# Four edits to the opening of a fused attention and feed-forward kernel: how the global index is spread, where the first scores stand, how the first feed-forward steps are cut, and where batch 1 is turned

## The chip, the core and the metric

The kernel runs on one core of a Trainium2 chip. A core has five engines that each work through their own list of instructions in order: TensorE (PE, matrix products; its weight loads are shown as PEld), VectorE (DVE), ScalarE (ACT), GpSimd (POOL) and SyncE (SP, which here only issues DMA transfers). They meet at semaphores. The metric is device time in microseconds (us); lower is better. The time before is 401.11 us, the median of four runs (398.67 to 401.29).

## What is computed

The reference is an attention with a window and a few global positions, then a gated feed-forward. Batch, heads, sequence and head size are 8, 8, 576 and 64.

```python
mask = np.abs(pos[:, None] - pos[None, :]) <= 32
is_global[global_idx] = True                        # 8 positions of 576
mask = mask | is_global[:, None] | is_global[None, :]
scores = np.where(mask, q @ k.T / sqrt(64), -1e9)
x = softmax(scores) @ v                             # as 4608 tokens x 512
g, val = x @ w_gate, x @ w_val                      # 512 -> 1536
ffn = (gelu(g) * val) @ w_out                       # 1536 -> 512
out = x + sigmoid(x @ w_res) * ffn
```

All inputs are float32 and `global_idx` is int64; the kernel multiplies in bf16 and accumulates in float32.

## The kernel before

**Tiling.** The 4608 tokens are cut into nine chunks of 512 (`NCH`), each of four token tiles of 128. A chunk is also eight windows of 64 queries, of which nine make a batch. For each chunk the feed-forward has twelve steps (`NFF`), one for each 128 columns of the hidden size: `ffn_in(c, j)` multiplies `xt` (the chunk with its features on the partitions) by a piece of `wg_t` and of `wv_t` into two PSUM banks (line 605), ACT takes the Gelu (611) and DVE multiplies and writes `ht` (612). Then `ffn_out` makes for each token tile the gate `r_ps` (623) and the product `f_ps` with `wo_t` in three thirds (648).

**Attention.** A window's scores are `kt` times `qt` (512, helper `heads`), ACT's exp writes `pt` (519, `weigh`), and `local_values` multiplies `pt` by `ve` or `vo`, the values of even and odd windows (552). `values` adds the part of the global keys, `gt` times `vgs` (564), and DVE divides into `xtok` (570 to 578). `turn_x` transposes a token tile of `xtok` on PE and copies it to `xt` (587, 588). `values` works on two banks of the pool `psm` where `split(c, t)` holds, else on the one two-bank tile of `psn`. The global rows take `kgz` and `qgz` (global keys and queries), `global_scores` (464, 469), `global_exp` (475 to 478), and `global_rows` (487 to 494), which ends in `vgs`.

**The opening.** For batches 0 and 1 keys and queries are loaded as float32, cast to `k_st` and `q_st`, and turned on PE by `turn_pair(b, p, what)` for head pairs p = 0 to 3 and for the tail of the sequence (p = -1); PE transposes (443) and DVE (k) or ACT (q) copies the result out (448, 450). For batch 0 the global columns are picked by products with one-hot tiles (`pick`, 409), and `spread_picked` (415) puts them into `kgz` and `qgz`. `first_scores(quad, pp)` adds the window mask by a product with `ident_big` (501) and then makes the scores. The index `global_idx` is loaded by ACT's queue into `gia` on all 128 partitions (line 173), copied to `gall` by DVE (312), and from there come `gpc`, `idx` (which GpSimd's gathers use, 320), `hot` and the one-hot tiles.

**Loads and casts.** The weights come as 20 pieces of 512 KB through staging slots (`load_piece`, issued by SP at 142) and are cast by GpSimd (`cast_piece`, 145). Several slots are tiles of batch 1 that are not yet in use. SP issues in this order: raw q and k of batch 0, v of batch 0 (185), ten pieces, two more, raw q and k of batch 1 (163, 167), two pieces, v of batch 1, six pieces. GpSimd casts in the same order and between the last pieces shifts v of batch 1 on chip (`shift_on_chip`, 107 and 108).

**Order.** The order of the work on each engine is written out by hand: the list from line 668 on for chunk 0, then the loop over chunks, in which `if c == 0` ... `elif j == ...` puts other work between the twelve steps. Buffers come from rotating pools: `psm` has four PSUM banks, `pss` two, `psn` one tile of two. An instruction waits where it stands, and what is behind it on its engine waits too. Before the change, the first two feed-forward steps of chunk 0 are split into two halves of 256 tokens (736 to 745); batch 1's turns stand after steps 8 to 11, two of them together after step 11 (796 to 798); `double_qk` and `turn_globals` of batch 1 stand after steps 2 and 3.

Of the kernel before, what the change touches and what calls it, by code (L numbers as in the profile page):

```python
# [8 lines left out]
F32 = mybir.dt.float32  # L9
# [14 lines left out]
def kernel(  # L24
# [129 lines left out]
    ht32 = ht.rearrange("p a b -> p (a b)").bitcast(F32)  # L154
    wo32 = wo_t.rearrange("p a b -> p (a b)").bitcast(F32)
    raw = [{"q": ht32, "k": wo32}, {"q": vraw.rearrange("p a b -> p (a b)"), "k": wo32}]
    gia = const.tile([128, 2 * NG], I32, name="gia", tag="gia")
    g32 = global_idx.bitcast(I32)

    def load_raw(b, what, p, eng):  # L160
# [9 lines left out]
    for p in (0, 1, -1, 2, 3):  # L170
        load_raw(0, "k", p, nc.sync)
        if p == 0:
            nc.scalar.dma_start(gia, bass.AP(tensor=g32.tensor, offset=g32.offset, ap=[[0, 128], [1, 2 * NG]]))
        load_raw(0, "q", p, nc.scalar if p in (0, 1) else nc.sync)

    def v_rows(c):
# [129 lines left out]


    idx = const.tile([128, B // 2], I32, name="idx", tag="idx")
    gall = const.tile([128, NG], F32, name="gall", tag="gall")
    mine8 = const.tile([128, NG], F32, name="mine8", tag="mine8")  # L310
    gpc = const.tile([128, 1], F32, name="gpc", tag="gpc")
    nc.vector.tensor_copy(gall, view(gia, 0, 128, 0, [[2, NG]]))
    nc.vector.tensor_tensor(mine8, gall, low8, ALU.mult)
    nc.vector.reduce_sum(gpc, mine8, axis=mybir.AxisListType.X)
    nc.vector.scalar_tensor_tensor(idx[:, 0:1], hrow, float(S), gpc, ALU.mult, ALU.add)
# [164 lines left out]
    def global_rows(b):  # L480

        e = b % 2
        sn = psn.tile([128, 2, 512], F32, name="sn", tag="nd")
        for c in range(-1, 5):
            for p in range(NP):
                if c < 0:
                    nc.tensor.matmul(sn[32 * p:32 * p + 32, 0, 0:2 * VG], own[e][:, 32 * p:32 * p + 32],
                                     view(vgb, 0, 128, (b // 2) * VG, [[0, 2], [1, VG]]), start=True, stop=False)
                else:
                    nc.tensor.matmul(sn[32 * p:32 * p + 16, 0, 0:2 * VG], ptg[e][:, c, 16 * p:16 * p + 16],  # L490
                                     ve[e][:, c, 2 * p:2 * p + 2, :], start=False, stop=(c == 4))
        nc.vector.tensor_tensor(view(vgs, 0, 128, e * H * VG, [[2 * VG, NP], [VG, 2], [1, VG]]),
                                view(sn, 0, 128, 0, [[0, NP], [VG, 2], [1, VG]]),
                                view(head8, 0, 128, 0, [[2, NP], [1, 2], [0, VG]]), ALU.mult)
# [40 lines left out]
        return mask  # L535

    def split(c, t):
        return c == 0 and t != 2

    def local_values(c, t):  # L540
        if split(c, t):
# [46 lines left out]
        (nc.vector.tensor_copy if c or t == 3 else nc.scalar.copy)(mine, tx)  # L588


    def ffn_in(c, j):
        steps = ffn_steps(c, j)
        for what in "gv":
            steps[what](0, 512)
        steps["end"]()

    def ffn_steps(c, j):
# [89 lines left out]
    first_scores(0, 0)  # L687
    for p in (-1, 2, 3):
        for what in "kq":
            turn_pair(0, p, what)  # L690
        for what in "kq":
            pick(p, what)
        if p < 0:
            ACT(found_end, isg[:, 0, 320:448])
    spread_picked()
    sg, ss = global_scores(0)
    row_masks()
    for c in range(2):
        cast_v(0, c, POOL)
    POOL(vo[0][64:128, 0:1, :, :], ve[0][0:64, 1:2, :, :])  # L700
    DVE(vo[0][0:64, 0:2, :, :], ve[0][64:128, 0:2, :, :])
    global_exp(0, sg, ss)
    first_scores(0, 1)
    cast_v(0, 2, POOL)
    POOL(vo[0][64:128, 1:2, :, :], ve[0][0:64, 2:3, :, :])
    for c in (3, 4):
        cast_v(0, c, POOL)
    spread_v(0, 1)
    first_scores(1, 0)
    POOL(vo[0][64:128, 2:4, :, :], ve[0][0:64, 3:5, :, :])  # L710
    first_scores(1, 1)
    begun_v = [local_values(0, t) for t in range(2)]
# [15 lines left out]
        load_piece(n)  # L728
    values(0, 0, begun_v[0])
    values(0, 1, begun_v[1])  # L730
    turn_x(0, 0)
    values(0, 2)
    turn_x(0, 1)
    values(0, 3)
    begun = [ffn_steps(0, j) for j in range(2)]
    begun[0]["g"](0, 256)
    begun[0]["v"](0, 256)
    turn_x(0, 2)
    begun[1]["g"](0, 256)
    turn_x(0, 3)  # L740
    begun[1]["v"](0, 256)
    for steps in begun:
        for what in "gv":
            steps[what](256, 512)
        steps["end"]()

    for c in range(NCH):
# [7 lines left out]
        held = None  # L755
        for j in range(NFF):
            if c or j > 1:
                ffn_in(c, j)
            if c == 0:
                if j == 0:  # L760
                    mask_rows(0, NW)
                elif j == 1:
                    mask_rows(NW, NWM)
                    zero_k(1)
                elif j == 2:
                    zero_gt(1, nc.vector)
                    zero_globals(1)
                    for n in range(1, B // 2):
                        nc.vector.tensor_single_scalar(idx[:, n:n + 1], idx[:, 0:1], float(2 * H * S * n), ALU.add)
                    double_qk(0, 1)  # L770
                elif j == 3:
                    got = turn_globals(0, 1)
                    for what in "kq":
                        DVE(compact[what][:, 0:1, :], got[what])
                elif j == 4:
                    spread_qk(1, compact, 0, {"k": DVE, "q": ACT})
                elif j == 5:
                    zero_v(1, nc.vector)
                    for p in (0, 1, 2, 3, -1):
                        for what in "kq":  # L780
                            cast_pair(1, p, what, POOL)
                    load_vraw(1)
                    for n in (14, 15):
                        load_piece(n)
                    for n in (12, 13):
                        cast_piece(n, POOL)
                    for c5 in range(5):
                        cast_v(1, c5, POOL)
                    for n in range(16, 20):
                        load_piece(n)  # L790
                    for i, n in enumerate(range(14, 20)):
                        cast_piece(n, POOL)
                        if i % 2:
                            shift_on_chip(i // 2)
                    shift_on_chip(3)
                for p in {8: (0,), 9: (1,), 10: (2,), 11: (3, -1)}.get(j, ()):
                    for what in "kq":
                        turn_pair(1, p, what)
            elif b < B:
                if c % 2 == 1:  # L800
                    n0, n1 = b // 2, b // 2 + 1
                    if j == 8:
                        double_qk(n0, n1)
                    elif j == 9:
                        got = turn_globals(n0, n1)
                        for what in "kq":
                            DVE(compact[what][:, n0:n1, :], got[what])
                        spread_v(n0, n1)
                if j == 8:
                    shift_v(b)  # L810
                    if b + 1 < B:
                        load_qk(b + 1)
                if j == 9:
                    spread_qk(b, compact, (b // 2) * 128, {"k": DVE, "q": DVE})
                if j == 11:
                    held = global_scores(b)
# [89 lines left out]
```

## Time and profile before

| | |
|---|---|
| median of four runs | 401.11 us (398.67 to 401.29) |
| the profiled execution | 398.9 us |
| its span, first to last instruction | 397.2 us |
| granted TensorE clock | 1.000 |
| DVE, ACT, POOL busy | 51%, 42%, 43% of the span |
| moved by DMA | 52.79 MB, mean 133 GB/s |
| chain that ended last | PE 80%, DMA 11%, POOL 3% |

Busy time by stretch, from the profile:

| us from the start | PE busy | DVE | ACT | POOL | DMA GB/s |
|---|---|---|---|---|---|
| 0 to 6 | 0.00 | 2.94 | 3.18 | 3.03 | 150 |
| 10 to 16.5 | 5.49 | 4.95 | 3.73 | 5.02 | 228 |
| 20 to 24 | 2.71 | 1.60 | 3.95 | 3.32 | 349 |
| 24 to 30 | 5.65 | 3.69 | 2.43 | 4.72 | 385 |
| 30 to 40 | 9.58 | 7.95 | 3.91 | 8.00 | 368 |
| 40 to 54 | 12.57 | 7.53 | 7.38 | 9.85 | 233 |
| 54 to 66 | 10.98 | 8.65 | 7.69 | 9.88 | 303 |
| 75 to 397 | 314.85 | 153.97 | 127.90 | 115.57 | 99 |

In a row of the timeline stand the start in us, the duration in us, the engine, the line of the kernel, the operation, what is written and what is read, with partitions and elements. In brackets follows for how long the engine was idle before it and what ended that. In the page's 40 slices each digit is the busy share of a slice in tenths. The chain that ended last is followed back from the last instruction; its rows have a start, a duration and a name.

### The profile page before, as it was taken

Reading aid. Unit: us, or ns where it says so; the run is one execution under the profiler, and the core shown is the slowest. Engines: PE = TensorE matmul, PEld = TensorE weight load, DVE = VectorE, ACT = ScalarE, POOL = GpSimd, SP = SyncE. Lnnn points to the kernel's source line nnn. Section 1 sums busy time; section 2 is a strip of 40 time slices with the busy share of each in tenths; the row PEclk is TensorE's granted clock in tenths of the full one; section 3 lists DMA queues with packets and bytes.
Section 4 is the critical chain, followed back from the end, with each engine's and each line's share of the span. In section 5 each row is a group of like instructions: output and inputs, shape, how many; then the busy total and the mean of one; then the engine's idle time right before and its main releaser. Section 6 shows DMA issues by size and latency. Waiting matters only on the chain.

```text
span 397.2 us, 8378 instructions
## 1 busy us (share of the span) xinstructions
PE 376.6 (95%) x3275; PEld 196.5 (49%) x3326; DVE 202.7 (51%) x444; ACT 168.6 (42%) x279; POOL 171.6 (43%) x207
## 2 busy tenths in 40 slices
PE   2889989999999999999999999999999999999995
PEld 1664545444544455445544554455445544554443
DVE  6857558435734464356444553665445534553322
ACT  5663484236433542345334623372337333633320
POOL 6777679768147613561297126712501210121011
PEclk9999999999999999999999999999999999999999
DMA  7999999999939982999399929993990310031002
GB/s 202 230 370 368 250 306 227 182 149 167 89 102 124 199 87 80 142 171 109 81 134 181 116 79 118 190 99 84 111 148 21 88 53 2 2 92 55 0 29 79
DMA packets 153144, 52.79 MB, mean 133 GB/s; under 512 B 136528, under 2 KB 143568, under 8 KB 153104
## 3 DMA queue, kind: packets, MB, share of 16 engines
q1 hardware_dynamic: 77024, 41.88, 46.5%
q0 software_dynamic: 75392, 9.84, 41.3%
q8 instruction: 26, 0.43, 0.5%
q10 hardware_dynamic: 688, 0.53, 0.5%
q14 instruction: 14, 0.11, 0.1%
HBM read 39.20 MB, written 9.44 MB: 122 GB/s over the span
## 4 chain that ended last, share of the span: by engine, by line
PE 80%; DMA 11%; POOL 3%; SPq 2%; issue 2%; ACT 1%; DVE 0%; DVEq 0%; POOLq 0%
PE v_ps L605 21%; PE f_ps L648 21%; PE g_ps L605 20%; PE r_ps L623 6%; PE nd L552 4%; DMA extra<-in_moe_w_val_dram 3%; DMA xtok<-in_moe_w_val_dram 2%; DMA vraw<-in_moe_w_out_dram 2%; PE sc L512 2%; DMA extra<-in_moe_w_res_dram 2%; PE nd L564 2%; SPq L185 2%; DMA wo_t<-in_k_dram 2%; PE ss L469 1%; POOL wo_t L145 1%
## 5 line engine op out<-in xcount | busy, mean ns | idle before, releaser
L612 DVE SCALAR_TENSOR_TENSOR ht<-gsb,v_ps 128x512 bf16<-128x512 bf16 x108 | 74.3, 688 | 99.5 <-PE v_ps L605 91.4
L611 ACT ACTIVATE gsb<-g_ps 128x512 bf16<-128x512 f32 x108 | 64.5, 597 | 127.3 <-PE g_ps L605 115.7
L654 POOL TENSOR_TENSOR ob<-prb,xtok 128x512 f32<-128x512 f32 x35 | 40.3, 1152 | 175.4 <-DVE prb L652 173.2
L605 PE MATMUL v_ps<-xt,wv_t 128*128 128x512 bf16 (+1 forms) x440 | 111.2, 375 | 0.5
L605 PE MATMUL g_ps<-xt,wg_t 128*128 128x512 bf16 (+1 forms) x422 | 108.8, 375 | 0.6
L648 PE MATMUL f_ps<-wo_t,ht 128*128 128x512 bf16 x395 | 98.1, 379 | 1.8 <-issue 0.8
L605 PEld LDWEIGHTS <-wv_t 128*128 128x128 bf16 x440 | 43.0, 98 | 50.2
L605 PEld LDWEIGHTS <-wg_t 128*128 128x128 bf16 x440 | 42.6, 98 | 48.8 <-DVE xt L588 0.4
L648 PEld LDWEIGHTS <-ht 128*128 128x128 bf16 x420 | 38.8, 98 | 38.6
L626 ACT ACTIVATE rsb<-r_ps 128x512 bf16<-128x512 f32 x36 | 21.7, 607 | 71.0 <-PE r_ps L623 69.9
L519 ACT ACTIVATE pt<-sc 128x512 bf16<-128x512 f32 x72 | 37.4, 624 | 4.4 <-PE sc L512 4.4
L652 DVE SCALAR_TENSOR_TENSOR prb<-rsb,f_ps 128x512 f32<-128x512 bf16 x35 | 24.0, 686 | 28.0 <-PE f_ps L648 25.6
L623 PE MATMUL r_ps<-wr_t,xt 128*128 128x512 bf16 x136 | 36.2, 379 | 0.5
L534 DVE TENSOR_TENSOR pt<-pt,maskw 128x512 bf16<-128x512 bf16 x64 | 29.0, 468 | 8.3 <-ACT pt L519 6.3
L91 POOL DMA_DIRECT2D q_st<-in_q_dram x25 | 21.4, 862 | 19.5 <-DMA qt<-q_st 19.4
L552 PEld LDWEIGHTS <-pt 128*128 128x128 bf16 x576 | 22.1, 97 | 9.3 <-issue 0.9
L99 POOL DMA_DIRECT2D ve<-in_v_dram x30 | 25.4, 864 | 0.0
L577 DVE TENSOR_TENSOR xtok<-nd,rden 128x512 bf16<-128x512 f32 x33 | 22.8, 691 | 1.3
L91 POOL DMA_DIRECT2D k_st<-in_k_dram x25 | 21.1, 856 | 5.4 <-DMA kt<-k_st 4.7
L552 PE MATMUL nd<-ve,pt 128*128 128x65 bf16 x320 | 22.7, 193 | 0.1
L576 DVE RECIPROCAL rden<-nd 128x8 f32<-128x8 f32 x33 | 6.8, 207 | 28.1 <-PE nd L564 27.9
L623 PEld LDWEIGHTS <-xt 128*128 128x128 bf16 x144 | 13.4, 97 | 15.1
(162 smaller groups left out, 299.4 us busy)
## 6 DMA issues: line engine op xcount, KB each, us to landing
out_dram<-ob SPq DMA_DIRECT2D x35, 256.0 KB
vo<-ve SPq DMA_DIRECT2D x12, 260.0 KB
q_st<-in_q_dram POOLq DMA_DIRECT2D x20, 128.0 KB, 5.3
k_st<-in_k_dram POOLq DMA_DIRECT2D x20, 128.0 KB, 6.5
ve<-in_v_dram POOLq DMA_DIRECT2D x18, 128.0 KB, 7.6
wo_t<-in_k_dram SPq DMA_DIRECT2D x8, 256.0 KB
vraw<-in_q_dram SPq DMA_DIRECT2D x8, 256.0 KB
extra<-in_moe_w_out_dram SPq DMA_DIRECT2D x4, 512.0 KB
```

Source lines behind the costliest of these rows:

```text
L91: nc.gpsimd.dma_start(dst[0:n, r, :].rearrange("p (h d) -> p h d", d=D), src[b].rearrange("h s d -> s h d")[128 * r:128 * r + n])
L99: nc.gpsimd.dma_start(t[p0:p1, c, :, 0:D], v[b].rearrange("h s d -> s h d")[s0 + p0:s0 + p1])
L519: nc.scalar.activation(mine, sc, ACTF.Exp, bias=0.0, scale=SCALE)
L534: nc.vector.tensor_tensor(m, m, view(maskw, 0, 128, 64 * i0, [[0, 2], [64, 4], [1, 64]]), ALU.mult)
L552: nc.tensor.matmul(nds[h // 4][:, VG * (h % 4):VG * (h % 4) + VG], view(pt, 0, 128, c0, [[1, 128]]), vw, start=(h % 4 == 0 and e == 0), st ...
L605: nc.tensor.matmul(held[what][:, c0:c1], w[:, kk, 128 * j:128 * j + 128], x[:, kk, c0:c1], start=(kk == 0), stop=(kk == NKT - 1))
L611: nc.scalar.activation(gsb, held["g"], ACTF.Gelu, bias=0.0, scale=1.0)
L612: nc.vector.scalar_tensor_tensor(ht[:, j, :], gsb, 0.5, held["v"], ALU.mult, ALU.mult)
L623: nc.tensor.matmul(r_ps, xt[c % 2][:, kk, 128 * t:128 * t + 128], wr_t[:, kk, :], start=(kk == 0), stop=(kk == NKT - 1))
L648: nc.tensor.matmul(held["f"], ht[:, j, 128 * t:128 * t + 128], wo_t[:, j, :], start=(j == 0), stop=(j == NFF - 1))
L652: nc.vector.scalar_tensor_tensor(prb, held["r"], 1.0, held["f"], ALU.add, ALU.mult)
L654: nc.gpsimd.tensor_tensor(ob, prb, xtok[c % 2][:, t, :], ALU.add)
```

## The change

It has four parts. The index is loaded as one row of 64 bytes; two masks split each value into its low three bits and the rest, DVE casts both to bf16 (each is exact there), and two products with the first row of `sel`, which is all ones, add them up on all 128 partitions. `first_scores(1, 0)` moves up, behind the turn of the tail; for pair 3 the picks and `spread_picked` stand before the turn; the row masks and the copy of the global values change places; `global_rows(0)` takes its bank from `pss`, and tiles 1 and 3 of chunk 0 use the tile of `psn`. Steps 0 and 1 of chunk 0 are made a token tile at a time: all four products of tile t follow directly on `turn_x(0, t)`. In the loop of chunk 0 the turns of batch 1 stand one after each of steps 7 to 10 and the last between the two products of step 11; the casts of the global keys and queries stand after step 4 and their transposes after step 6, and `zero_v` after step 3.

```diff
--- before.py
+++ after.py
@@ -154,7 +154,7 @@
     ht32 = ht.rearrange("p a b -> p (a b)").bitcast(F32)
     wo32 = wo_t.rearrange("p a b -> p (a b)").bitcast(F32)
     raw = [{"q": ht32, "k": wo32}, {"q": vraw.rearrange("p a b -> p (a b)"), "k": wo32}]
-    gia = const.tile([128, 2 * NG], I32, name="gia", tag="gia")
+    gia = const.tile([1, 2 * NG], I32, name="gia", tag="gia")
     g32 = global_idx.bitcast(I32)
 
     def load_raw(b, what, p, eng):
@@ -170,7 +170,7 @@
     for p in (0, 1, -1, 2, 3):
         load_raw(0, "k", p, nc.sync)
         if p == 0:
-            nc.scalar.dma_start(gia, bass.AP(tensor=g32.tensor, offset=g32.offset, ap=[[0, 128], [1, 2 * NG]]))
+            nc.scalar.dma_start(gia, bass.AP(tensor=g32.tensor, offset=g32.offset, ap=[[2 * NG, 1], [1, 2 * NG]]))
         load_raw(0, "q", p, nc.scalar if p in (0, 1) else nc.sync)
 
     def v_rows(c):
@@ -306,10 +306,18 @@
 
 
     idx = const.tile([128, B // 2], I32, name="idx", tag="idx")
+    gs = const.tile([1, 2, NG], I32, name="gs", tag="gs")
+    g2 = const.tile([1, 2, NG], BF16, name="g2", tag="g2")
     gall = const.tile([128, NG], F32, name="gall", tag="gall")
     mine8 = const.tile([128, NG], F32, name="mine8", tag="mine8")
     gpc = const.tile([128, 1], F32, name="gpc", tag="gpc")
-    nc.vector.tensor_copy(gall, view(gia, 0, 128, 0, [[2, NG]]))
+    for n, keep in enumerate((7, 1023 - 7)):
+        nc.vector.tensor_single_scalar(gs[:, n, :], view(gia, 0, 1, 0, [[2, NG]]), keep, ALU.bitwise_and)
+    nc.vector.tensor_copy(g2, gs)
+    gp = psm.tile([128, NG], F32, name="gp", tag="mm")
+    for n in range(2):
+        nc.tensor.matmul(gp, sel[0:1, :], g2[:, n, :], start=(n == 0), stop=(n == 1))
+    nc.vector.tensor_copy(gall, gp)
     nc.vector.tensor_tensor(mine8, gall, low8, ALU.mult)
     nc.vector.reduce_sum(gpc, mine8, axis=mybir.AxisListType.X)
     nc.vector.scalar_tensor_tensor(idx[:, 0:1], hrow, float(S), gpc, ALU.mult, ALU.add)
@@ -480,14 +488,17 @@
     def global_rows(b):
 
         e = b % 2
-        sn = psn.tile([128, 2, 512], F32, name="sn", tag="nd")
+        if b:
+            sn = psn.tile([128, 2, 512], F32, name="sn", tag="nd")[:, 0, 0:2 * VG]
+        else:
+            sn = pss.tile([128, 2 * VG], F32, name="sn", tag="sc")
         for c in range(-1, 5):
             for p in range(NP):
                 if c < 0:
-                    nc.tensor.matmul(sn[32 * p:32 * p + 32, 0, 0:2 * VG], own[e][:, 32 * p:32 * p + 32],
+                    nc.tensor.matmul(sn[32 * p:32 * p + 32, :], own[e][:, 32 * p:32 * p + 32],
                                      view(vgb, 0, 128, (b // 2) * VG, [[0, 2], [1, VG]]), start=True, stop=False)
                 else:
-                    nc.tensor.matmul(sn[32 * p:32 * p + 16, 0, 0:2 * VG], ptg[e][:, c, 16 * p:16 * p + 16],
+                    nc.tensor.matmul(sn[32 * p:32 * p + 16, :], ptg[e][:, c, 16 * p:16 * p + 16],
                                      ve[e][:, c, 2 * p:2 * p + 2, :], start=False, stop=(c == 4))
         nc.vector.tensor_tensor(view(vgs, 0, 128, e * H * VG, [[2 * VG, NP], [VG, 2], [1, VG]]),
                                 view(sn, 0, 128, 0, [[0, NP], [VG, 2], [1, VG]]),
@@ -535,7 +546,7 @@
         return mask
 
     def split(c, t):
-        return c == 0 and t != 2
+        return c == 0 and t % 2 == 0
 
     def local_values(c, t):
         if split(c, t):
@@ -588,10 +599,12 @@
         (nc.vector.tensor_copy if c or t == 3 else nc.scalar.copy)(mine, tx)
 
 
-    def ffn_in(c, j):
+    def ffn_in(c, j, between=None):
         steps = ffn_steps(c, j)
         for what in "gv":
             steps[what](0, 512)
+            if what == "g" and between:
+                between()
         steps["end"]()
 
     def ffn_steps(c, j):
@@ -687,26 +700,33 @@
     first_scores(0, 0)
     for p in (-1, 2, 3):
         for what in "kq":
-            turn_pair(0, p, what)
+            if p == 3:
+                pick(p, what)
+            else:
+                turn_pair(0, p, what)
+        if p == 3:
+            spread_picked()
         for what in "kq":
-            pick(p, what)
+            if p == 3:
+                turn_pair(0, p, what)
+            else:
+                pick(p, what)
         if p < 0:
             ACT(found_end, isg[:, 0, 320:448])
-    spread_picked()
+            first_scores(1, 0)
     sg, ss = global_scores(0)
-    row_masks()
     for c in range(2):
         cast_v(0, c, POOL)
     POOL(vo[0][64:128, 0:1, :, :], ve[0][0:64, 1:2, :, :])
     DVE(vo[0][0:64, 0:2, :, :], ve[0][64:128, 0:2, :, :])
+    spread_v(0, 1)
+    row_masks()
     global_exp(0, sg, ss)
     first_scores(0, 1)
     cast_v(0, 2, POOL)
     POOL(vo[0][64:128, 1:2, :, :], ve[0][0:64, 2:3, :, :])
     for c in (3, 4):
         cast_v(0, c, POOL)
-    spread_v(0, 1)
-    first_scores(1, 0)
     POOL(vo[0][64:128, 2:4, :, :], ve[0][0:64, 3:5, :, :])
     first_scores(1, 1)
     begun_v = [local_values(0, t) for t in range(2)]
@@ -728,20 +748,21 @@
         load_piece(n)
     values(0, 0, begun_v[0])
     values(0, 1, begun_v[1])
+    begun = [ffn_steps(0, j) for j in range(2)]
+
+    def begin(t):
+        for steps in begun:
+            for what in "gv":
+                steps[what](128 * t, 128 * t + 128)
+
+    values(0, 2)
     turn_x(0, 0)
-    values(0, 2)
-    turn_x(0, 1)
     values(0, 3)
-    begun = [ffn_steps(0, j) for j in range(2)]
-    begun[0]["g"](0, 256)
-    begun[0]["v"](0, 256)
-    turn_x(0, 2)
-    begun[1]["g"](0, 256)
-    turn_x(0, 3)
-    begun[1]["v"](0, 256)
+    begin(0)
+    for t in range(1, 4):
+        turn_x(0, t)
+        begin(t)
     for steps in begun:
-        for what in "gv":
-            steps[what](256, 512)
         steps["end"]()
 
     for c in range(NCH):
@@ -755,7 +776,7 @@
         held = None
         for j in range(NFF):
             if c or j > 1:
-                ffn_in(c, j)
+                ffn_in(c, j, (lambda: [turn_pair(1, -1, what) for what in "kq"]) if c == 0 and j == 11 else None)
             if c == 0:
                 if j == 0:
                     mask_rows(0, NW)
@@ -767,15 +788,16 @@
                     zero_globals(1)
                     for n in range(1, B // 2):
                         nc.vector.tensor_single_scalar(idx[:, n:n + 1], idx[:, 0:1], float(2 * H * S * n), ALU.add)
+                elif j == 3:
+                    zero_v(1, nc.vector)
+                elif j == 4:
                     double_qk(0, 1)
-                elif j == 3:
+                elif j == 6:
                     got = turn_globals(0, 1)
                     for what in "kq":
                         DVE(compact[what][:, 0:1, :], got[what])
-                elif j == 4:
                     spread_qk(1, compact, 0, {"k": DVE, "q": ACT})
                 elif j == 5:
-                    zero_v(1, nc.vector)
                     for p in (0, 1, 2, 3, -1):
                         for what in "kq":
                             cast_pair(1, p, what, POOL)
@@ -793,9 +815,9 @@
                         if i % 2:
                             shift_on_chip(i // 2)
                     shift_on_chip(3)
-                for p in {8: (0,), 9: (1,), 10: (2,), 11: (3, -1)}.get(j, ()):
+                if 7 <= j < 11:
                     for what in "kq":
-                        turn_pair(1, p, what)
+                        turn_pair(1, j - 7, what)
             elif b < B:
                 if c % 2 == 1:
                     n0, n1 = b // 2, b // 2 + 1
```

In the listing of each engine's instructions SP and POOL keep their order. PE has 68 more instructions: the two products of the index and 32 more of the first two steps, each with its weight load. DVE has two more rows and ACT the same work in another order.

## The prediction

> **What bounds the kernel now.** I read the page first (engine shares, 40 slices, the chain that ended last), then the chain in order of time up to 76 us, then the timeline to 75 us.
>
> ```profile
> span 397.2 us, 8378 instructions
> PE 376.6 (95%) x3275; PEld 196.5 (49%) x3326; DVE 202.7 (51%) x444; ACT 168.6 (42%) x279; POOL 171.6 (43%) x207
> PE   2889989999999999999999999999999999999995
> DMA  7999999999939982999399929993990310031002
> ```
>
> After 75 us the kernel is matrix work back to back (PE busy 314.85 of 322.00 us there) and the change touches none of it, so all that can move is the moment at which PE gets there. Before 75 us the 16 DMA engines are full too. The chain in order of time says which of the two ends last:
>
> ```profile
> 17.08 9.05 DMA xtok<-in_moe_w_val_dram
> 26.19 11.18 DMA extra<-in_moe_w_val_dram
> 39.88 7.38 DMA extra<-in_moe_w_res_dram
> 52.13 8.59 DMA vraw<-in_moe_w_out_dram
> 60.77 1.05 POOL wo_t L145
> 66.39 0.63 POOL vo L108
> 67.02 0.59 PE f_ps L648 x2
> ```
>
> The loads set the pace to 60.7 us, GpSimd's casts and shifts from there to 67.0, and only then PE. PE itself is close behind that: it starts the last values tile of chunk 1 (which reads what L108 shifted) at 67.69, 0.67 us after POOL was done at 67.02. That gap is how much PE can gain if loads and POOL stay put. Other edges are looser: the last `wo_t` cast ends at 65.60, its product starts at 66.57 (0.97 to spare).
>
> The places that the change touches, from the timeline:
>
> ```profile
> 4.75 0.17 DVE L312 CAST gall<-gia 128x8 f32<-128x8 int32 x1 [1.69 <-DMA gia<-in_global_idx_dram]
> 10.57 1.01 PE L501 MATMUL sc<-xt,ident_big 128*128 128x512 bf16 x2
> 17.40 0.59 PE L501 MATMUL sc<-xt,ident_big 128*128 128x512 bf16 x2
> 20.41 0.61 POOL L190 CAST ve<-vraw 96x512 bf16<-96x512 f32 x1 [1.14 <-DMA vraw<-in_v_dram]
> 21.97 0.70 DVE L492 TENSOR_TENSOR vgs<-sn,head 128x520 bf16<-128x520 f32 x1 [2.28 <-PE sn L490]
> 22.73 0.61 PE L564 MATMUL nd<-vgs,gt 128*128 128x260 bf16 x4 [0.81 <-DVE vgs L492]
> 25.70 0.58 ACT L588 COPY xt<-tx 128x512 bf16<-128x512 bf16 x1 [0.51 <-PE tx L587]
> 28.77 0.33 PEld L605 LDWEIGHTS <-wg_t 128*128 128x128 bf16 x4 [0.36 <-DVE xt L588]
> 34.51 0.10 PEld L399 LDWEIGHTS <-kgd 128*128 128x128 bf16 x1 [0.86 <-DVE kgd L389]
> 51.15 0.38 PE L443 MATMUL tk<-ident,k_st 128*128 128x128 bf16 x4 [0.67 <-ACT qt L450]
> 52.70 0.31 PE L464 MATMUL sg<-qt,kgz 128*32 128x288 bf16 x4 [0.60 <-ACT qt L448]
> ```
>
> In brackets stands the idle time before an instruction and what ended it. DVE waits for the index; PE waits for the global rows (0.81), for a turned tile (0.36), for a cast on DVE, and twice for ACT when batch 1 is turned.
>
> **Index row.** Removed: 127 of 128 rows of 64 bytes. Added: two masks of 1x8 and one cast on DVE, two 8-column products on PE, and the copy now reads PSUM. The landing of one row isn't in the trace. Upper bound: as now, 4.75. Lower: the last output piece takes 1.71 us from issue to landing, and the index is issued by 1.23, so 2.94. The Trainium skill (DMA: Bandwidth & Descriptors, Anatomy of one DMA) puts a fixed 2.0 us on a transfer, an estimate of 3.23 here. DVE is free at 3.06, so row or rule differ by 0.17 us at most; I take 3.06. The small steps of this chain follow each other at 0.20 (4.75, 4.95, 5.15), a second mask adds 0.08: cast at 3.34, PE at 3.55, product about 0.2, copy at 3.8 instead of 4.75. So 0.95 us sooner; if the row lands as late as now, 0.75 later. Behind that wait on DVE stand all masks and the first k cast (7.21), on POOL the gathers. What follows: q's last pair is cast at 12.93 as its load lands, and v's last piece at 20.41, also a load. So the 0.95 is mostly swallowed. The index rows also trickle through the ramp of the loads (31, 138, 269 GB/s in the three 0.75 us slices from 2.25 us, against 381 after): without them the whole stream of loads may be 0 to 0.7 us ahead; I take 0.3.
>
> **First scores reordered.** Eight exps, the same products, other places. Scores of quad 1, half 0, move from 18.3 us to about 12.5. Here the trace and a rule speak against it: the two 512-column products take 1.01 us at 10.57 and 0.59 at 17.40. TensorE: Matmul & The Clock Gate (Part 1) says that the array runs at half rate until about 3.4 us of sustained activity. Issue to issue the moved block costs 0.95 + 0.54 us early and 0.87 late (18.27 to 19.14), so 0.6 more than it saves, unless PE would wait there anyway. Late, 0.87 goes from the path: `nd` could start at 19.15 instead of 20.02; but it needs the two exps behind the global exps, which end at 19.5 now. I take 19.5, 0.5 sooner. `sn` moves to another bank and ends 0.4 to 0.6 sooner; it can't end before v's last cast (21.02 now, 20.7 with the stream 0.3 ahead) plus 0.25. So the global products, 22.73 now (call that G), come 0.6 to 1.0 sooner: 0.7. On DVE the row masks (0.76 + 0.74) now stand behind the v copies; the masked `gt` is needed only at G.
>
> **A token tile at a time.** This is the cost. PE is in order, and each turn now stands directly before the steps that read it. Turn to first product takes 1.07 us by ACT (four transposes 0.39, hand-over 0.04, copy 0.58, 0.06) and 0.91 by DVE (27.86 to 28.77). 32 products of 256 columns become 64 of 128. The four transposes at 69.42 take 0.22, so 55 ns each with their weight load; the skill's page on TensorE (Back-to-back issue gap) gives about 81 ns for such pairs at 128 columns. By the row the four tiles are 4 x 0.87 = 3.5 us, as now; by the rule 5.2, 1.7 us more. I take the row. From G: global products and tile 2 to +1.2; tile 3 needs the bank that tile 1 holds until DVE is done (0.30 + 1.11 + 0.94 = +2.35), then 0.75, so tile 0's steps run +3.1 to +4.0. Then 1.07 + 0.87, 1.07 + 0.87, 0.91 + 0.87 = 5.66: step 2 starts at G + 9.65. Now it is 30.53 - 22.73 = G + 7.80. So **1.85 us lost** on PE, at G 0.7 gained: step 2 starts 1.15 later than now. Weights don't stop it: the last of the first four pieces is cast at 27.22.
>
> **Globals of batch 1 two steps later.** PE's hole is from 33.98 (step 3 done) to 34.72: 0.74, of which the two transposes are 0.11 to 0.2. The DVE casts (0.99 + 0.21) now have two steps of time. **0.55 gained.** The ones and zeros of v (0.09 + 0.28 + 0.28) only trade places on DVE; four banks cover that, and the cast that frees the buffer ends at 33.04.
>
> **Turns of batch 1.** Now: step 10 ends at 47.70, r_ps starts at 53.45, 5.75 us. After: turn 0.44, g 0.86, last turn 0.44 (+0.1 for its bank), v 0.86, ACT's tail copies 0.74 mostly under v, then 0.62 + 0.5 for the global scores: 3.75. One turn more lies before step 10: 0.44. **1.55 gained.** The casts are ready: pair 0 at 39.62, its turn not before 41.4. But ACT now does the last Gelu (0.60) behind those copies and before the table load and the exps; relative to r_ps it falls behind by 0.9 - 0.5 = 0.4, and PE already waits for ACT's exps at 57.44 (0.17). **0.4 given back**; bounds 0 and 0.6.
>
> No DMA or POOL instruction changes its place on SP or POOL.
>
> **Sum.** -0.7 + 1.85 - 0.55 - 1.55 + 0.4 = -0.55 at PE, about -0.85 if the earlier stream passes through at G in full. The lid at 67 us is 0.67 + 0.3 = 1.0. I take -0.7: the profiled execution of 398.9 (its span 397.2 and 1.7 around it) would be 398.2. The runs shown have a median of 401.11 and spread from 398.67 to 401.29, more than this whole effect, so on the median: **400.4 us**.
>
> **Rivals.** (1) The turned tiles decide (slower). If ACT's exps hold PE at 57 us whatever the turns save, the 1.55 is gone: -0.7 + 1.85 - 0.55 + 0.4 = +1.0, so 402.1. For it: three exposed copies in strict order; against: the two holes of 0.67 and 0.60 stand in the trace and have named causes. It decides once less than 0.55 of the 1.55 arrives; at 81 ns per product it would be worse, +2.7. (2) The loads move more: without index rows the stream is 0.7 ahead, POOL is done at 66.3, G comes 1.4 sooner, ACT keeps up. PE's sum is -1.4 + 1.85 - 0.55 - 1.55 = -1.65, the lid 0.67 + 0.7: -1.4, so 399.7; with the array warm one window sooner and a median near the lowest runs, 398.5. (3) It does nothing at the end: loads and casts hold PE at 67.6 as now, 401.1, within 0.3; the holes only move. Against: POOL ends 0.67 before PE.
>
> **Chances.** Small gain 0.50 (399.8 to 400.9), turned tiles 0.18, earlier stream 0.20, nothing 0.12. The range of 398.3 to 402.3 covers them but for the ends of rivals 1 and 2 and takes in the spread of the runs. Half a per cent, 2.0 us, is about what a measurement of this kernel can tell from no change. Faster by more needs rival 2 and a low median: 0.22. Slower by more needs rival 1 with dear products: 0.10. Within: 0.68.
>
> **What would show it.** `gall` at about 3.8; G near 22.0; three waits of PE of 0.7 to 0.85 us on turned tiles, with step 2 at about 31.7; no wait at the globals' transposes; r_ps near 52.3; then PE at the last values tile at 66.7 to 67.1 with POOL just done. It is wrong if the 128-column products exceed 55 ns, if ACT holds the scores of chunk 1, or if the casts land much sooner.

## The result and the profile after

| | before | after |
|---|---|---|
| median | 400.01 us (63 runs, 398.65 to 401.78) | 398.73 us (42 runs, 397.23 to 400.23) |
| ratio | | 0.9968 [0.9959, 0.9978] |
| the profiled execution | 398.9 us | 399.54 us |
| its span | 397.2 us | 397.8 us |

The change saves 1.28 us, 0.32% of the time (0.22 to 0.41%): real, and below the half per cent that the prediction called measurable. The two profiled executions point the other way by 0.64 us. Before's lies near the lower end of its runs and after's 0.8 us above its median, so spans must not be subtracted here; stages can be compared one by one. The runs of before gather near 399 and near 401 us, and the profiled one is of the first kind: of the 71 runs of before beside the experiments below, the 22 with a granted clock of 1.000 average 398.98 us and the other 49 average 400.75, while for after 12 and 32 such runs average 398.79 and 398.80, so most of the 1.28 us is gained over runs of which there is no profile.

The page of after, its first lines:

```profile
span 397.8 us, 8446 instructions
PE 377.4 (95%) x3309; PEld 197.2 (50%) x3360; DVE 202.2 (51%) x445; ACT 168.6 (42%) x279; POOL 172.1 (43%) x207
PE   3979998999999999999999999999999999999995
DMA  8999999899739972999299929993990310041002
```

The first slice (10 us) has PE at 3 and DMA at 8 tenths, where it was 2 and 7: the opening begins sooner. From 75 us on the slices look alike, but not all is equal there: chunk 1 takes 41.15 us (40.59 in before) and chunk 4 takes 41.04 (40.69), which is where nearly all of the 0.64 us the other way comes from. The account of the prediction comes back to chunk 4.

The timeline of after at the places shown of before (start, duration, engine, line; in brackets the idle time before and what ended it):

```profile
3.71 0.17 DVE L320 COPY gall<-gp 128x8 f32<-128x8 f32 x1 [0.28 <-PE gp L319]
12.29 1.04 PE L512 MATMUL sc<-xt,ident_big 128*128 128x512 bf16 x2
18.49 0.87 POOL L190 CAST ve<-vraw 96x512 bf16<-96x512 f32 x1 [0.81 <-DMA vraw<-in_v_dram]
21.66 0.61 PE L575 MATMUL nd<-vgs,gt 128*128 128x260 bf16 x4 [0.80 <-DVE vgs L503]
24.06 0.20 PE L563 MATMUL nd<-ve,pt 128*128 128x65 bf16 x1 [0.56 <-DVE xtok L588]
26.73 0.38 PE L618 MATMUL g_ps<-xt,wg_t 128*128 128x128 bf16 x4 [0.67 <-ACT xt L599]
28.68 0.38 PE L618 MATMUL g_ps<-xt,wg_t 128*128 128x128 bf16 x4 [0.67 <-ACT xt L599]
30.47 0.38 PE L618 MATMUL g_ps<-xt,wg_t 128*128 128x128 bf16 x4 [0.52 <-DVE xt L599]
39.95 0.10 PEld L407 LDWEIGHTS <-kgd 128*128 128x128 bf16 x1
51.32 0.43 PE L472 MATMUL sg<-qt,kgz 128*32 128x288 bf16 x8
53.73 0.62 PE L523 MATMUL sc<-qt,kt 64*128 64x64 bf16 x31 [0.38 <-ACT ptg L483]
```

The index is there at 3.71 instead of 4.75, v's last cast starts at 18.49 instead of 20.41 and the global products (G) at 21.66 instead of 22.73. At 24.06 PE waits 0.56 us for the bank that tile 1 of chunk 0 holds; then three turned tiles each hold PE for 0.52 to 0.67 us where before had one wait of 0.36. PE's waits for the globals' transposes and for ACT in batch 1's turns are gone; behind `r_ps` there is a new one of 0.38 for ACT's exps. Stage by stage, with the shift against before in each profiled execution:

| moment, us | before | after | shift | change within the stage |
|---|---|---|---|---|
| `gall` | 4.75 | 3.71 | -1.04 | |
| G | 22.73 | 21.66 | -1.07 | -0.03 |
| step 2 | 30.53 | 31.54 | +1.01 | +2.08 |
| `r_ps` of chunk 0 | 53.45 | 52.19 | -1.26 | -2.27 |
| first `f_ps` | 59.34 | 58.62 | -0.72 | +0.54 |
| third values tile of chunk 1, second half | 65.93 | 65.79 | -0.14 | +0.58 |
| feed-forward of chunk 1 | 74.88 | 74.74 | -0.14 | 0.00 |

Of the 1.26 us that PE is ahead at `r_ps`, 1.12 are gone fourteen microseconds later. The chain that ended last, in order of time, names the place. In after it runs through DVE's masks (`pt` times `maskw`, line 545), no longer through the loads and GpSimd:

```profile
26.09 0.59 ACT xt L599
63.47 2.28 DVE pt L545 x2
65.79 0.36 PE nd L563 x6
```

### The profile page after: what moved, and what is told of

It is laid out like the page before. It is cut to its first block, busy times and chain, and to the rows that moved or that the text cites. A ratio compares the mean times of both kernels' runs of the same rounds, so it can differ in the third digit from the quotient of the medians.

```text
span 397.8 us, 8446 instructions
## 1 busy us (share of the span) xinstructions
PE 377.4 (95%) x3309; PEld 197.2 (50%) x3360; DVE 202.2 (51%) x445; ACT 168.6 (42%) x279; POOL 172.1 (43%) x207
## 4 chain that ended last, share of the span: by engine, by line
PE 76%; DMA 7%; issue 5%; DVE 4%; POOL 4%; ACT 2%; DVEq 0%; POOLq 0%
PE v_ps L618 19%; PE g_ps L618 18%; PE f_ps L661 18%; PE r_ps L636 6%; PE nd L563 4%; DMA kgf<-in_k_dram,idx 2%; PE sc L523 2%; POOL ve L99 2%; PE nd L575 2%; DMA kt<-k_st 2%; DMA out_dram<-ob 1%; POOL ob L667 1%; DMA vgf<-in_v_dram,idx 1%; PE ss L477 1%; ACT pt L530 1%
## 5 line engine op out<-in xcount | busy, mean ns | idle before, releaser
L618 PEld LDWEIGHTS <-wg_t 128*128 128x128 bf16 x456 | 43.4, 98 | 50.3 <-issue 2.4
L563 PE MATMUL nd<-vo,pt 128*128 128x65 bf16 x256 | 20.1, 193 | 1.4 <-DVE pt L545 0.9
```

The costliest lines, as they stand in the source:

```text
L563: nc.tensor.matmul(nds[h // 4][:, VG * (h % 4):VG * (h % 4) + VG], view(pt, 0, 128, c0, [[1, 128]]), vw, start=(h % 4 == 0 and e == 0), st ...
L618: nc.tensor.matmul(held[what][:, c0:c1], w[:, kk, 128 * j:128 * j + 128], x[:, kk, c0:c1], start=(kk == 0), stop=(kk == NKT - 1))
```

## The experiments

Each kernel is after with one thing undone or added, or before with one part alone. Medians are from 6 or 12 runs (seven for the first kernel with casts on ACT); us in brackets are what the ratio differs from 1, times 400.0. The kernels ran in three groups, each with its own runs of before (medians 400.54, 399.44 and 400.60), so ratios are compared and not medians. The medians of before move more from group to group than its averages (400.26, 400.02 and 400.57), so between kernels of different groups some tenths of a microsecond can come from before itself.

**The index alone** (before with that part):

```diff
-    gia = const.tile([128, 2 * NG], I32, name="gia", tag="gia")
+    gia = const.tile([1, 2 * NG], I32, name="gia", tag="gia")
...
-    nc.vector.tensor_copy(gall, view(gia, 0, 128, 0, [[2, NG]]))
+        nc.tensor.matmul(gp, sel[0:1, :], g2[:, n, :], start=(n == 0), stop=(n == 1))
+    nc.vector.tensor_copy(gall, gp)
```

> The kernel before with the index row alone. The changed kernel measures 1.28 us less than before. If the loads set the time (its load stream stood 1.1 to 1.4 us ahead), this edit alone gives most of that: about -1.0 us, ratio 0.9975, with GpSimd's casts of the first weights 1.4 us sooner. If PE's own sum decides, as in the prediction, the index gives only what reaches the global products: -0.3 to -0.7 us, and the turns must give the rest.

398.45 us, ratio 0.995 [0.9933, 0.9967] (-2.0). At best estimate one small part alone gains more than the whole change; the intervals overlap a little.

**All but the index** (after, the same lines reversed):

> The changed kernel with the index loaded on 128 partitions as before. Loads decide: the gain is nearly gone, 0 to -0.3 us against before. PE's sum decides: turns and globals still pay for the token tiles, about -0.6 us against before.

399.93 us, ratio 0.999 [0.9972, 1.0008]. The other three parts together are worth nothing that can be told from zero. In the trace `gall` is at 4.98, G at 22.66.

How an index of 64 bytes does this stands in the DMA view from 1.5 to 5 us (40 slices of 0.0875 us: busy share of the DMA engines in tenths, then GB/s). Before, and then after:

```profile
DMA  0000000000009601242224566466689989999999
GB/s 0 0 0 1 7 2 1 2 4 3 4 15 51 38 25 51 72 85 76 73 64 144 189 202 190 165 191 202 226 294 309 342 306 363 363 375 386 375 363 375
```

```profile
DMA  0000977966338999978898899998988899989799
GB/s 0 0 1 0 47 47 117 187 187 117 117 129 293 339 374 363 328 246 281 304 328 293 304 351 398 328 363 316 328 316 304 304 351 340 304 281 293 269 316 316
```

With 128 rows of 64 bytes the keys and queries issued at the same time hardly move until 2.5 us, and 300 GB/s are passed at 4.1. With one row that is at 2.6. Half a megabyte has landed at 4.81 before and 3.68 after, 8 MB at 29.74 and 28.30, 16 MB at 56.55 and 55.16: the whole stream is 1.1 to 1.4 us ahead and stays so. Without the index part 8 MB is at 29.72, and in the profiles of all twelve kernels with the one row it is 0.9 to 2.6 us sooner than in before, so that part is the cause of the earlier stream. In addition SP's wait of 0.8 us for `gia`, which held a load of q until 4.74, is gone. Why the first packets of k come 0.6 us later beside the rows, no view shows. The same edit also brings `gall` a microsecond sooner, and no run parts the two; that the stream is what pays is argued from the chain of before, which runs through the loads.

**All but the token tiles** (after, the first two steps as before, and tile 1 and 3 in their old banks):

```diff
-        return c == 0 and t % 2 == 0
+        return c == 0 and t != 2
...
-    begin(0)
-    for t in range(1, 4):
-        turn_x(0, t)
-        begin(t)
+    begun[0]["g"](0, 256)
+    begun[0]["v"](0, 256)
+    turn_x(0, 2)
+    begun[1]["g"](0, 256)
+    turn_x(0, 3)
+    begun[1]["v"](0, 256)
```

> The changed kernel with the first two feed-forward steps in halves of 256 tokens and tiles 1 and 3 of chunk 0 on the banks of before. The prediction prices the token tiles at 1.85 us of PE. If PE ends last, this is 1.85 us faster than the changed kernel (-3.1 us against before, ratio 0.992). If GpSimd's casts and shifts and the DVE masks at 63 to 67 us are a lid, at most 0.3 us faster than the changed kernel, because that kernel already waits there.

396.26 us, ratio 0.9889 [0.9866, 0.9913] (-4.4): the fastest of all. From G to step 2 it takes 7.80 us, exactly as before and as with the index alone; after takes 9.88.

**All but the turns and globals of batch 1** (after, batch 1 as before):

```diff
-                if 7 <= j < 11:
+                for p in {8: (0,), 9: (1,), 10: (2,), 11: (3, -1)}.get(j, ()):
                     for what in "kq":
-                        turn_pair(1, j - 7, what)
+                        turn_pair(1, p, what)
```

> The changed kernel with batch 1's turns after steps 8 to 11 and its global casts and transposes after steps 2 and 3, as before. The prediction prices these two at 0.55 + 1.55 - 0.4 = 1.7 us. If PE ends last, 1.7 us slower than the changed kernel (+0.4 us against before). If the lid holds, PE has 0.6 us in hand there, so 1.1 us slower than the changed kernel (-0.2 us against before).

400.15 us, ratio 0.9997 [0.9978, 1.0016]: this part is worth 1.2 us within the change (0.3 to 2.0). `r_ps` comes at 53.80, 1.6 later than in after.

**Token tiles turned one ahead** (after):

```diff
+    turn_x(0, 1)
     begin(0)
-    for t in range(1, 4):
-        turn_x(0, t)
-        begin(t)
+    turn_x(0, 2)
+    begin(1)
+    turn_x(0, 3)
+    begin(2)
+    begin(3)
```

> The changed kernel with each turn one tile ahead: the turn of tile t + 1 stands before the products of tile t, so PE no longer waits for the copy. If the token tiles cost what they do through the three exposed copies (0.67 + 0.67 + 0.52 us of idle PE), this gives about 1.9 us against the changed kernel, ratio to before 0.992, step 2 at about 29.6 us. If it is the 128-column products themselves, or the banks of tiles 1 and 3, it gives under 0.5 us.

397.21 us, ratio 0.9943 [0.9922, 0.9965] (-2.3). The timeline of PE in this kernel, a turn and the products after it:

```profile
25.88 0.39 PE L598 MATMUL tx<-ident,xtok 128*128 128x128 bf16 x4
26.10 0.39 PE L618 MATMUL g_ps<-xt,wg_t 128*128 128x128 bf16 x4
```

Four transposes take 0.22 us and no bracket follows: all three waits are gone, and G to step 2 is 7.54 us. The products of 128 columns are not dear, 0.22 for four; it was the exposed copies. The wait of 0.56 for the bank stays. In time the gain over after is 1.0 us, with intervals that overlap a little (the medians lie 1.5 apart).

**All but the first scores** (after, the list up to the last first score as before):

```diff
         if p < 0:
             ACT(found_end, isg[:, 0, 320:448])
-            first_scores(1, 0)
...
+    spread_v(0, 1)
+    first_scores(1, 0)
```

> The changed kernel with the scores of quad 1, the picks of pair 3, the row masks and the value copy in the order of before. From the sum of the parts measured so far (index, turns, token tiles) this part is worth about nothing: within 0.5 us of the changed kernel. If the early block costs what the slow array makes of it, this is 0.6 us faster; if taking 0.87 us from in front of the values is on the path, 0.5 us slower.

400.48 us, ratio 1.0005 [0.9984, 1.0026]. By that the part is worth 1.5 us (0.6 to 2.4), but the traces do not show it: chunk 1 starts at 74.67 here and at 74.74 in after. The profiled run of this kernel, 399.27 us, is the second quickest of its twelve.

**Index and turns alone** (the two edits last named, both taken back):

> Only the index row and the turns of batch 1, with the first scores and the first steps as before. Index and turns by their own runs: -2.0 and -0.9 to -1.4 us, so about -3 us, ratio 0.9925. If the first scores are worth the 1.5 us that no_first showed, this is 1.5 us slower than the kernel without the tiles (0.9889), which also gives 0.9925; if it is 0.989 here, the first scores are worth nothing and index and turns add up to more than each alone.

396.95 us, ratio 0.9908 [0.9888, 0.9929] (-3.7). Against all but the tiles (-4.4) the first scores are worth 0.8, with an interval from -0.5 to +2.0.

These kernels make a ladder:

| parts in the kernel | us against before | the step |
|---|---|---|
| index | -2.0 | -2.0 (± 0.7) |
| index, turns and globals | -3.7 | -1.7 (± 1.1) |
| index, turns and globals, first scores | -4.4 | -0.8 (± 1.3) |
| all four | -1.3 | +3.2 (± 1.0) |

The last step compares two groups. Straight from the medians, 396.26 and 398.73, it is 2.5 us.

**Two casts of `w_out` on ACT.** What takes PE's lead back between 58 and 66 us? These runs take work from GpSimd, where the prediction had put the lid.

```diff
-                        cast_piece(n, POOL)
+                        if n < 18:
+                            cast_piece(n, POOL)
...
+            for n in (18, 19):
+                cast_piece(n, ACT)
             cast_second("k", 0, NQT, ACT)
```

> The changed kernel with the last two pieces of w_out cast by ACT, which is idle at 60 to 63 us, and not by GpSimd. In the changed kernel the masks at 63.47 take 2.27 us for two while GpSimd casts, and 0.82 for two while it is idle. If GpSimd beside DVE is what gives PE's lead back between 62 and 66 us, these masks take about 1.0 us and chunk 1's feed-forward starts about 0.6 us sooner: ratio to before 0.995. If the lead is lost elsewhere, no change against the changed kernel; ACT's later casts of k may then cost up to 0.5 us.

402.62 us, ratio 1.0073 [1.0044, 1.0102]: slower than before by 2.9. In this kernel and the next the casts stand behind the loads of batch 2, so 64 rows of one piece of `w_out` are taken from the keys of batch 2. That order is also what they cost; ACT in the timeline, and DVE's masks at the same time:

```profile
66.63 1.99 ACT L145 CAST wo_t<-extra 128x1024 bf16<-128x1024 f32 x2 [6.54 <-DMA extra<-in_k_dram]
```

```profile
64.10 0.75 DVE L545 TENSOR_TENSOR pt<-pt,maskw 128x512 bf16<-128x512 bf16 x2
```

ACT idles 6.54 us for a load, and the products wait 2.3 us for its casts. But the two masks now take 0.75 us, with GpSimd idle.

**The same without token tiles:**

> The changed kernel without the token tiles and with the last two casts on ACT. Without the tiles alone it measured 396.26 us, 0.9889 of before. In that one PE goes from the second pair of values at 59.85 to the third at 64.42, 4.57 us where the kernel before needs 3.21. If GpSimd beside DVE does that, another 0.8 to 1.2 us go: ratio 0.986. If not, 0.989.

402.44 us, ratio 1.005 [1.003, 1.0071]. The same delay; chunk 1 starts at 79.11.

**The casts on ACT ahead of those loads** (after):

```diff
+            for n in (18, 19):
+                cast_piece(n, ACT)
             for what in "kq":
                 load_second(what)
-            for n in (18, 19):
-                cast_piece(n, ACT)
             cast_second("k", 0, NQT, ACT)
```

> The changed kernel with the last two pieces of w_out cast by ACT, now ahead of the loads of batch 2 on SP. In act_casts and no_tiles_act those loads stood ahead: ACT's casts waited for them until 66.63, and 64 rows of one piece were taken from k of batch 2. If GpSimd beside DVE gives back PE's lead between 62 and 66 us, the masks at 63.5 take about 1.0 instead of 2.27 us for two and chunk 1's feed-forward starts 0.6 to 1.2 us sooner: ratio 0.994. If not, 0.9968 as the changed kernel; slower than that if ACT is late again.

398.33 us, ratio 0.995 [0.9931, 0.9968] (-2.0). Against after it is 0.7 us faster at best estimate, with intervals that overlap. What happens to the masks: before, then after, then this kernel (timelines of GpSimd, DVE and PE; line 534 of before is 545 of after):

```profile
63.31 2.29 POOL L145 CAST wo_t<-extra 128x1024 bf16<-128x1024 f32 x2
64.28 1.59 DVE L534 TENSOR_TENSOR pt<-pt,maskw 128x512 bf16<-128x512 bf16 x2
65.93 0.20 PE L552 MATMUL nd<-vo,pt 128*128 128x65 bf16 x1 [0.38 <-DVE pt L534]
```

```profile
63.25 2.22 POOL L145 CAST wo_t<-extra 128x1024 bf16<-128x1024 f32 x2
63.47 2.27 DVE L545 TENSOR_TENSOR pt<-pt,maskw 128x512 bf16<-128x512 bf16 x2
65.79 0.20 PE L563 MATMUL nd<-vo,pt 128*128 128x65 bf16 x1 [0.94 <-DVE pt L545]
```

```profile
61.95 0.61 POOL L107 COPY vo<-ve 64x520 bf16<-64x520 bf16 x1
62.61 0.71 POOL L108 COPY vo<-ve 64x520 bf16<-64x520 bf16 x1
62.19 1.42 DVE L545 TENSOR_TENSOR pt<-pt,maskw 128x512 bf16<-128x512 bf16 x2
```

DVE begins 0.81 us sooner in after than in before and is done 0.13 sooner: it ends 0.27 us after GpSimd's pair of casts in both. All the lead becomes wait at the masks. Beside two of GpSimd's copies of 0.61 and 0.71 (the last kernel) two masks take 1.42, beside two casts 2.27, beside nothing 0.75.

**The same on the two faster kernels** (without tiles, and turned one ahead):

> The same edit on the changed kernel without token tiles (0.9889 of before without it, with 1.5 us of PE waiting for masked scores at 56 to 75 us and 0.3 for a cast on GpSimd). If those waits come from GpSimd's casts, 0.8 to 1.5 us less: ratio 0.986. If not, 0.989 or more.

396.95 us, ratio 0.9907 [0.9889, 0.9926]; without ACT's casts 0.9889 [0.9866, 0.9913]: no gain. PE's longest wait from 55 us on in this kernel, next to the wait for the masks that all but the tiles has up to 75 us (what waited, for what; us in all, times, longest):

```profile
PE f_ps L661 <- POOL wo_t L145: 1.5, 1, 1.5
```

```profile
PE nd L563 <- DVE pt L545: 1.5, 2, 0.9
```

An earlier cast, still GpSimd's, takes the place of the masks as the longest wait.

> The same edit on the changed kernel with each turn one tile ahead (0.9943 of before, interval 0.9922 to 0.9965, its profiled run 394.8 us of span against 397.8). If the masks hold its lead back, 0.8 to 1.5 us less: ratio 0.991. If not, 0.994.

396.61 us, ratio 0.9909 [0.9887, 0.9931]; without ACT's casts 0.9943 [0.9922, 0.9965]. Chunk 1 starts at 71.67, the soonest of all, against 72.22. So in none of the three kernels is the gain in time from taking the two casts off GpSimd clear of the noise; what the runs show is how long the masks take.

## Why the prediction was right, and where it was not

The change of time was put at -0.7 us and is -1.28 (0.9968 [0.9959, 0.9978]), within half a per cent. The 400.4 us was reckoned from a median of four runs, 401.11; with 63 runs before is 400.01, so as a time the forecast is 1.7 us off and 398.73 lies below the likeliest case (399.8 to 400.9), while as a difference it is just inside it. Most of the signs came as listed: `gall` at 3.71 (3.8), step 2 at 31.54 (31.7), `r_ps` at 52.19 (52.3), three waits on turned tiles, none at the globals' transposes. PE's sum held too: -0.55 forecast, -0.72 at the first `f_ps`.

The match is in part luck. Two terms, one of each sign, were too small in the times, and their errors partly cancel. In the profiled pair only 0.14 us of PE's lead reaches chunk 1, because the lid was misread; where the rest of the 1.28 of the medians arises, no profile shows.

**Index: failed in size.** The path to `gall` held to the tenth: DVE's first step on the index starts at 2.99, the copy at 3.71 where 3.8 was said. The 3.23 that the fixed 2.0 us gave was too late: the row was in use at 2.99, 1.64 us after the end of its issue and 2.17 after the beginning. (The section behind the 2.0 us describes transfers that GpSimd issues; this one is ACT's.) The step that failed is "the whole stream of loads may be 0 to 0.7 us ahead; I take 0.3". It measured 1.1 to 1.4, and the index alone gives 2.0 us. The row-by-row rates of before (31, 138, 269 GB/s) had been read as a slow ramp and charged to the index only in small part; the run without the index part has the slow ramp again (`gall` at 4.98, 8 MB at 29.72). The 0.7 for G, with the first scores in it, stands against 2.8 for these two steps of the ladder. Inside the full change less of it arrives: all but the index is only 0.9 us slower than after (± 0.8).

**First scores: open.** The masks' two products at 12.29 take 1.04 us, as the row of 10.57 had said, so moving them costs PE what was charged. Their worth in time is 1.5 by one pair of kernels and 0.8 by the other, the second not distinct from zero.

**Token tiles: mechanism right, too small.** Three exposed copies at 0.67, 0.67 and 0.52, tile 3 at G + 2.40 where + 2.35 was forecast for the bank, and 2.08 us at step 2 where 1.85 was. Row against rule came out for the row: 0.22 for four products, not the 0.32 of the 81 ns in the Trainium skill (TensorE: Matmul & The Clock Gate, Back-to-back issue gap). The ladder says 3.2 (± 1.0), the medians 2.5. Of what goes beyond 2.08, part lies behind 75 us (below).

**Turns and globals: right.** -0.55 - 1.55 + 0.4 = -1.7; the ladder has -1.7, and the run without this part 1.2. In the trace step 10's end to `r_ps` takes 3.66 us (3.75 forecast, 5.75 before), and 0.54 is given back before `f_ps` (0.4 forecast), 0.38 of it in the new wait for ACT's exps.

**The lid: right place, wrong reading.** "That gap is how much PE can gain if loads and POOL stay put", 0.67, is wrong. PE does not end at GpSimd's shifts but at DVE's masks, which share the time with GpSimd's casts; it already waited 0.38 for them in before, a bracket that the prediction did not read. With casts at the same moment (63.25 and 63.31) PE gained 0.14 of the 1.26 it was ahead, the same 0.13 by which the masks were done sooner. The Trainium skill has a rule for it (SBUF — State Buffer, Who interferes with whom): a DVE instruction with two inputs in SBUF waits out a GpSimd instruction that reads SBUF. The rows agree: two masks take as long as the two casts or copies beside them (2.27 and 2.22; 1.42 and 0.61 + 0.71), and 0.75 when GpSimd is idle. That the shared port is the reason is the page's account; the rows show the durations only. How much this costs in an execution hangs on when the loads bring the last casts. In the profile of after this pair starts at 63.25, for the second piece of `w_out` came late:

```profile
57.02 1.04 POOL L145 CAST wo_t<-extra 128x1024 bf16<-128x1024 f32 x1 [1.41 <-DMA extra<-in_moe_w_out_dram]
```

In all but the turns that cast stands at 53.73. With the index alone the pair starts at 60.42: it falls beside the masks of the tile before (1.99 us for two), and PE's waits for masks come to 0.68, against 0.94 in after and 0.38 in before. So this one execution shows little of the gain that the runs measure; how the others lie cannot be seen.

**Behind 75 us: a term put at nothing.** The prediction said that the change touches nothing after 75 us, "so all that can move is the moment at which PE gets there". That does not hold. In the profiles of all eight kernels with token tiles PE stands still in chunk 4, always before the same product, the last of the global scores, which reads keys that a DMA has turned. The hole is 0.2 to 1.2 us long. In the six kernels without token tiles, before among them, there is none. Chunk 4 takes 40.86 to 41.86 us in the eight and 40.69 or 40.70 in the six. From after, the product, then two lines of the DMA view from 210 to 214 us (slices of 0.1 us):

```profile
219.10 0.26 PE L477 MATMUL ss<-qgz,kt 128*128 128x16 bf16 x4 [0.20 <-DMA kt<-k_st]
GB/s 95 184 269 416 170 179 20 10 8 23 3 79 287 292 156 360 151 148 145 150 154 143 148 151 195 205 229 246 219 119 9 10 9 8 10 9 10 128 151 145
q8 instruction: 1, 0.02, 1.7%
```

The last line is one load of 16 KB of instructions. It starts at 211.56, takes 1.08 us, and soon after it the DMA engines move next to nothing for 0.7 us (8 to 10 GB/s from 213.0), while the keys are being turned. (The pause before it, at 210.6, follows a load of 8 KB that the kernels of both kinds have there.) In all eight kernels this load starts 14.0 to 14.7 us into chunk 4; in the other six it starts at 23.4 to 23.9, after the product. The token tiles put 64 more instructions on PE (32 products, each with its weight load), so the places in its program where more has to be loaded come sooner. That this load causes the hole is argued from the pattern of the fourteen profiles; no run moves it alone.

**The rivals.** The earlier stream (rival 2) is the mechanism that held, at twice its size, and it decides the sign. That its 398.5 is near the 398.73 says little: it took in a warmer array and a low median, and is 399.7 without them. The turned tiles (rival 1) take 3.2 of 4.4 back, but ACT did not swallow the turns' gain, so the change stayed on the gaining side. "Nothing at the end" (rival 3) is out for the medians, but the profiled pair comes close to it: PE's last values tile starts at 67.55, where 66.7 to 67.1 was forecast and before has 67.69.

What beats both kernels: the change without its token tiles, 0.9889 [0.9866, 0.9913]; turned one ahead with two casts on ACT is as fast within the intervals, 0.9909. The kernel with turns one ahead reaches chunk 1 0.95 us sooner in its profile than the one without tiles (72.22 and 73.17) and is not faster by the runs. Of that, 0.45 goes in chunk 4 (41.14 and 40.69). The rest stays open; they ran in different groups, and the profiled run is the quickest of twelve for the first and the slowest of six for the second.

## What to carry to other kernels

Before a small load is written off as swallowed, look at the first microseconds of the DMA view: what it does to the large transfers issued beside it can outweigh its own latency. A piece of work cut finer must be paid for with a turn issued one piece ahead, or each hand-over stands open. And a lead on one engine is worth only what the next shared wait leaves of it: read PE's small brackets at the point where loads, casts and masks meet before naming the lid. A stage that an edit does not touch can still change: compare every chunk of the two profiles, the loads of instructions among them.

## What the runs showed of the hardware

- With 128 rows of 64 bytes beside the first loads the whole stream came later: 300 GB/s are passed at 4.1 us with them and at 2.6 with one row, and half a megabyte lands 1.13 us later.
- The one row of 64 bytes, issued by ACT from 0.82 to 1.35, was used by DVE at 2.99, so it landed at most 1.64 us after its issue ended; DVE had only then finished the work before it, so the landing itself is not seen.
- A mask of 128x512 bf16 on DVE takes 0.37 us with GpSimd idle, 0.71 beside GpSimd's copies and 1.13 beside its casts: two in 0.75, 1.42 and 2.27.
- Products of 128 columns with their weight load followed each other at 55 ns (four in 0.22 us).
- Chunks 1 to 6 take 40.6 to 40.8 us each, but now and then one takes 40.9 to 41.9, well behind the edit. That may make part of the spread of 3 us between runs of one kernel.
- A load of 16 KB of instructions took 1.08 us in chunk 4 of after, and nearly no data moved for 0.7 us soon after it. In eight of eight kernels where it falls among the transfers that turn keys, PE then waits 0.2 to 1.2 us for them; in six of six where it falls later, it does not.
